# The last two blocks of a chunk-attention and Mish kernel: g @ w_out by seven products of halves, in a phase of its own

## The chip, the cores and the metric

One Trainium2 chip, one of its cores. The metric is the device time of one execution in microseconds; the kernel before took 867.61 us, the median of three runs (866.41 to 867.76).

## The reference

Attention within chunks of 64 tokens, then a feed-forward layer with the Mish function, all in fp32:

```python
q_c = q.reshape(B, H, nc, chunk, D)          # 8, 8, 9, 64, 64; k_c and v_c alike
scores = scale * np.matmul(q_c, k_c.transpose(0, 1, 2, 4, 3))
scores = scores - np.max(scores, axis=-1, keepdims=True)
attn = np.exp(scores)
attn = attn / (np.sum(attn, axis=-1, keepdims=True) + 1e-09)
out = np.matmul(attn, v_c)
...
x = out.transpose(0, 2, 1, 3).reshape(4608, 512)
h = x @ w_in                                  # w_in 512 x 2048
g = h * np.tanh(softplus(h))                  # Mish
return g @ w_out                              # w_out 2048 x 512
```

## The kernel before

Every fp32 matrix operand is split into a high and a low part in the matmul's own format (fp32r), and a product is made of three: high by high, high by low, low by high. gh and gl are the two parts of g, A11 to S4 (in `ops_of`) those of w_in.

The 4,608 tokens go as 512 first tokens, by plain products, and then four blocks of 1,024 (m = 1 to 4; the code's QUADS). In a block the tokens are two sides of 512, and `unit(m, u)` does x @ w_in for 256 columns of w_in (u = 0 to 7), by seven products of halves in place of eight. Each product is 6 matmuls of 512 columns (L697). The sums of halves of x are made ahead by `x_step`, eleven pairs of steps per block. The operands of w_in lie in scratch memory (`wa_u`), one product's 256 KB at a time, and `load_op` fetches the next one into a ring of 5 tiles when a product has used one.

The seven products of a unit give h of both token sides, in PSUM tiles x, y and v. ACT and DVE copy, add and apply Mish. The first side's g is split at once (`g_split`), and its share of g @ w_out is put on a list, `fill`, as single matmuls of 512 columns (L450). `filled(n)` takes n of them off this list between the products, so that PE always has work. The second side's g is kept in `zb`, and `phase_two(m)` multiplies it with w_out behind the eight units: for each of 16 groups f of 128 rows of w_out, ACT casts gh, DVE subtracts gl, and PE does 12 matmuls, one group behind. In the meantime DVE and ACT make the next block's x. The attention of the next block's four pairs of 128-token tiles is laid into the units, a pair to two units.

w_out stays in SBUF, its high part in `wo_h` and its low part in `wo_l`. All instructions stand in the program's order on each engine (a manual schedule), and SP issues nearly all DMAs in that order.

A tile from a pool waits until the pool's buffer is released by all who use the tile before it. `c_p` has one buffer (8 KB per partition); the outputs of a block's sides also go through it.

Of the kernel before, what the change touches and what calls it, by code (L numbers as in the profile page):

```python
# [23 lines left out]
def kernel(  # L24
# [421 lines left out]
    def down_mm(key, f, d, t, n):  # L446
        if f == 0 and n == 0:
            acc[t] = ps_o.tile([P, DM], F32, name=f"o_{key}_{t}", tag=f"o{t}")
        g, w_ = ((d["gl"], wo_h), (d["gh"], wo_l), (d["gh"], wo_h))[n]
        nc.tensor.matmul(  # L450
            acc[t],
            lhsT=g[:, t * P : (t + 1) * P],
            rhs=w_[:, f],
            start=(f == 0 and n == 0),
            stop=(f == NF - 1 and n == 2),
        )
# [223 lines left out]
    wop = []  # L680

    def load_op():
        if len(wop) < len(ops):
            m, u, n = ops[len(wop)]
            t = wop_p.tile([P, 2, 2, P], F32R, name=f"w{m}_{u}_{n}", tag="w")
            nc.sync.dma_start(
                out=t.bitcast(F32).rearrange("p s k c -> p s (k c)"), in_=ops_of[u][:, OPS.index(n)]
            )
            wop.append(t)

    def product(m, u, n, o, start):
        t = wop[((m - 1) * NU + u) * len(PRODUCTS) + n]
        x = [xo[PRODUCTS[n][1]][:, part] for part in range(2)]
        i = 0
        for w_, x_ in ((0, 0), (1, 0), (0, 1)):
            for kt in range(2):
                nc.tensor.matmul(  # L697
                    o,
                    lhsT=t[:, w_, kt],
                    rhs=x[x_][:, kt],  # L700
                    start=(start and i == 0),
                    stop=(i == 5),
                    skip_group_check=not start,
                )
# [8 lines left out]
    for u in range(1, NU):  # L713
        for place, step, n in (
            ((u - 1, 2), s_adds, u),
            ((u - 1, 3), s_hi, u),
            ((u - 1, 4), s_lo, u),
            ((u - 1, 7), s_load, u + 1),
        ):
            BUILDS.setdefault(place, []).append((step, n))  # L720

    def unit(m, u):
        late = m == 1
# [70 lines left out]
        nc.scalar.copy(out=b2, in_=x)  # L794
# [28 lines left out]
    def phase_two(m):  # L823
# [7 lines left out]
        for f in range(NF):  # L831
# [16 lines left out]
            if f == 10 and m + 1 < QUADS:  # L848
                load_qk(first_pair(m + 2))

    with tc.manual_schedule():
# [10 lines left out]
        p = first_pair(QUADS)
        for t, n in enumerate((9, 6, 6, 3)):
            filled(n)
            store("last", (p + 1, p + 3), t, 2)


# [36 lines left out]
```

## Time and profile before

| what | value |
|---|---|
| median of three runs | 867.61 us |
| the profiled execution's own time | 868.13 us |
| its span | 866.0 us |
| PE busy | 823.5 us (95%), 5724 matmuls |
| DVE busy | 433.7 us (50%) |
| ACT busy | 380.9 us (44%) |
| HBM read, written | 108.00 MB, 28.31 MB |
| mean granted clock of PE | 0.987 |

A profile's times are microseconds from the start of the span. PE is the matmul engine, PEld its weight loads, which lie beside the matmuls; DVE is the vector engine, ACT the scalar engine, SP the queue that issues DMAs. A row of the timeline has start, length, engine, line, operation, out<-in, shape and count, and in brackets the idle time before it with what ended it. A row of the groups has the count, the busy time and the mean in ns of one.

### The profile page before, as it was taken

The page shows a single profiled execution, that of the slowest core. Times are in us where ns is not written, and L with a number is a line of the kernel's source. Part 1 is how long each engine was busy: PE and PEld are TensorE (multiplying, and loading weights), DVE is VectorE, ACT ScalarE, POOL GpSimd, SP SyncE. Part 2 cuts the span into 40 slices and gives each one's busy share as a digit, 9 for nine tenths or more (in the row PEclk, how much of TensorE's full clock was granted, in tenths as well). Part 3 has the DMA queues.
Part 4 walks back from the last instruction along what each step waited for, and adds up shares of the span by engine and source line. Part 5 has one row for each costly group of instructions (what it writes and reads, how often), then busy time and mean ns, then how long its engine had stood idle before and what let it go on. Part 6 is the DMA issues. An engine that isn't in the chain of part 4 may idle for free.

```text
span 866.0 us, 14086 instructions
## 1 busy us (share of the span) xinstructions
PE 823.5 (95%) x5724; PEld 669.8 (77%) x5724; DVE 433.7 (50%) x641; ACT 380.9 (44%) x547; POOL 0.7 (0%) x6
## 2 busy tenths in 40 slices
PE   4978989889999999999999999999999999999997
PEld 4757767568888888888888888888888888888885
DVE  6787878646465663343354635524437432223322
ACT  4768775444454453443443425434435232222321
POOL 0000000000000000000000000000000000000000
PEclk9889999999999999999999999999999999999999
DMA  7698774777777502645544216555432064444202
GB/s 279 246 307 313 274 248 161 245 256 251 255 237 250 145 1 84 202 141 173 158 144 110 61 50 208 146 174 156 139 104 50 1 177 126 119 117 131 49 1 50
DMA packets 71216, 137.24 MB, mean 158 GB/s; under 512 B 6896, under 2 KB 18160, under 8 KB 70128
## 3 DMA queue, kind: packets, MB, share of 16 engines
q1 hardware_dynamic: 70224, 135.29, 49.4%
q10 hardware_dynamic: 928, 1.05, 0.4%
q8 instruction: 46, 0.75, 0.3%
q14 instruction: 18, 0.15, 0.0%
HBM read 108.00 MB, written 28.31 MB: 157 GB/s over the span
## 4 chain that ended last, share of the span: by engine, by line
PE 81%; DVE 7%; DMA 5%; ACT 4%; issue 2%; SPq 1%; ACTq 0%; DVEq 0%
PE x L697 19%; PE v L697 10%; PE y L697 5%; DMA wst<-in_w_in 3%; PE av L228 2%; PE pt L296 2%; PE s L228 2%; DVE wc L128 2%; PE o_(1, 1)_0_2751 L450 1%; PE o_(3, 1)_0_5862 L450 1%; PE o_(2, 1)_0_4323 L450 1%; PE o_(4, 0)_1_6270 L450 1%; PE o_(4, 0)_2_6274 L450 1%; PE o_(2, 1)_2_4331 L450 1%; PE o_(1, 1)_1_2755 L450 1%
## 5 line engine op out<-in xcount | busy, mean ns | idle before, releaser
L697 PE MATMUL x<-x_T,w_S 128*128 128x512 f32 x384 | 99.3, 394 | 2.0 <-ACT zb L778 1.0
L438 DVE CAST gh<-z 128x512 fp32r<-128x512 f32 x72 | 30.6, 425 | 136.3 <-PE o_(4, 0)_3_6288 L450 42.1
L431 ACT ACTIVATE zb<-zb 128x512 f32<-128x512 f32 x64 | 40.4, 632 | 116.0 <-DVE zb L709 115.9
L697 PEld LDWEIGHTS x<-x_T,w_S 128*128 128x128 f32 x384 | 71.0, 188 | 18.2 <-ACT zb L778 1.4
L709 DVE TENSOR_TENSOR zb<-v,zb 128x512 f32<-128x512 f32 x64 | 43.9, 685 | 57.4 <-ACT zb L794 57.4
L709 DVE TENSOR_TENSOR z<-y,z 128x512 f32<-128x512 f32 x32 | 22.1, 692 | 89.4 <-PE y L697 89.4
L440 DVE TENSOR_TENSOR gl<-z,gh 128x512 fp32r<-128x512 f32 x80 | 55.4, 693 | 12.0 <-ACT gh L436 9.5
L794 ACT COPY zb<-x 128x512 f32<-128x512 f32 x32 | 18.8, 586 | 83.2 <-PE x L697 83.2
L697 PE MATMUL x<-x_T,w_A 128*128 128x512 f32 x192 | 49.4, 392 | 3.8 <-ACT zb L794 3.8
L697 PE MATMUL x<-x_B,w_A 128*128 128x512 f32 x192 | 50.4, 397 | 0.9 <-DVE x_B L373 0.7
L697 PE MATMUL y<-x_B,w_A 128*128 128x512 f32 x192 | 51.2, 402 | 0.0
L418 PE MATMUL h<-x_first,wi 128*128 128x512 f32 (+1 forms) x204 | 50.0, 399 | 1.0 <-ACT x_first L336 0.7
L697 PE MATMUL v<-x_B,w_S 128*128 128x512 f32 x192 | 49.2, 392 | 1.3 <-DVE zb L709 1.3
L697 PE MATMUL v<-x_T,w_S 128*128 128x512 f32 x192 | 48.9, 390 | 1.0 <-DMA w_S<-wa 1.0
L418 PEld LDWEIGHTS h<-x_first,wi 128*128 128x128 f32 x204 | 38.9, 204 | 9.3 <-ACT x_first L336 0.9
L431 ACT ACTIVATE z<-z 128x512 f32<-128x512 f32 x32 | 20.2, 631 | 58.4 <-DVE z L709 58.4
L697 PEld LDWEIGHTS x<-x_T,w_A 128*128 128x128 f32 x192 | 35.6, 188 | 13.2 <-ACT zb L794 5.9
L697 PEld LDWEIGHTS v<-x_B,w_S 128*128 128x128 f32 x192 | 35.7, 188 | 9.9 <-DVE zb L709 2.6
L697 PEld LDWEIGHTS v<-x_T,w_S 128*128 128x128 f32 x192 | 35.9, 188 | 9.1 <-issue 1.4
L697 PEld LDWEIGHTS x<-x_B,w_A 128*128 128x128 f32 x192 | 35.0, 188 | 8.8 <-DVE x_B L373 1.1
L697 PEld LDWEIGHTS y<-x_B,w_A 128*128 128x128 f32 x192 | 34.6, 188 | 9.1 <-DVE zb L709 1.8
L296 PE MATMUL pt<-ident,p 128*128 128x128 f32 x144 | 20.9, 290 | 13.7 <-DVE p L287 10.4
(296 smaller groups left out, 1726.4 us busy)
## 6 DMA issues: line engine op xcount, KB each, us to landing
w_S<-wa SPq DMA_DIRECT2D x128, 256.0 KB, 2.8
w_A<-wa SPq DMA_DIRECT2D x96, 256.0 KB, 2.8
v<-in_v SPq DMA_DIRECT2D x16, 512.0 KB, 4.9
wa<-a SPq DMA_DIRECT2D x8, 1024.0 KB, 4.8
wst<-in_w_out SPq DMA_DIRECT2D x7, 1024.0 KB, 5.4
wst<-in_w_in SPq DMA_DIRECT2D x6, 1024.0 KB, 6.2
wa<-wi SPq DMA_DIRECT2D x24, 256.0 KB, 4.1
q<-in_q SPq DMA_DIRECT2D x12, 512.0 KB, 4.1
```

Of the source, the lines that this page charges most:

```text
L128: nc.vector.scalar_tensor_tensor(out=c, in0=x, scalar=mask, in1=y, op0=op, op1=ALU.bitwise_or)
L228: nc.tensor.matmul(o[h * CHUNK : (h + 1) * CHUNK, c, t - ts.start, g], lhsT=l[rows, t, 2 * g + h], rhs=r[rows, t, 2 * g + h], start=True, ...
L296: nc.tensor.transpose(out=d["pt", ts.start][:, t - ts.start, g], in_=d["p"][:, t, g].rearrange("p c k -> p (c k)"), identity=ident,)
L418: nc.tensor.matmul(h[:, cols], lhsT=wi[i // 2][:, i % 2, w_, kt], rhs=x[:, x_, kt, cols], start=(n == 0), stop=(n == 3 * NK - 1),)
L431: nc.scalar.activation(out=out_, in_=in_, func=AF.Mish)
L438: nc.vector.tensor_copy(out=d["gh"], in_=z)
L440: nc.vector.tensor_tensor(out=d["gl"], in0=z, in1=d["gh"].bitcast(F32), op=ALU.subtract)
L450: nc.tensor.matmul(acc[t], lhsT=g[:, t * P : (t + 1) * P], rhs=w_[:, f], start=(f == 0 and n == 0), stop=(f == NF - 1 and n == 2),)
L697: nc.tensor.matmul(o, lhsT=t[:, w_, kt], rhs=x[x_][:, kt], start=(start and i == 0), stop=(i == 5), skip_group_check=not start,)
L709: nc.vector.tensor_tensor(out=z, in0=o, in1=z, op=ALU.add)
L794: nc.scalar.copy(out=b2, in_=x)
```

## The change

Blocks 1 and 2 go as before. In blocks 3 and 4 (`BOTH_FROM = 3`) g @ w_out, too, is made of seven products of halves, and no longer fills the gaps of x @ w_in:

- **Up phase**, `up_two(m, n)`: units 2n and 2n+1 are interleaved, product by product, 14 products of 6 matmuls; each unit has its own PSUM tiles x, y and v. The four quarters of g (G11, G12, G21, G22) and S1 stay in SBUF as 128 x 512 fp32 tiles, 40 of them. The attention of the next block is laid between the products at `beside(h)`.
- **Down phase**, `down_all(m)`: 56 steps, types 0 to 6 with 8 units each. `operand(k, u)`, called two steps ahead, makes the type's sum where it has one (S2 = S1 - G11 and S4 = G12 - S2, on DVE, in place), casts gh on ACT and subtracts gl on DVE; gh and gl have three buffers each. A step is 12 matmuls of 256 columns (L1060 of the new kernel). At the end of a type ACT or DVE takes the accumulated tile out, and DVE adds totals for the products that need two. The last block's last two steps are held back and done half by half, and ACT and DVE copy the last half together.
- **Operands of w_out**: made once, in block 2, for eight units: `t_whole` (DVE: high + low), `t_sums` (three on DVE), `t_hi` (ACT), `t_lo` (DVE, with a DMA of 1 MB to `wb_u`), and `t_keep` (three DMAs). `BUILDS_OUT` lays the four steps beside four products in a row; builds 0 to 2 and 5 to 7 start at the beginning of units 1 to 3 and 5 to 7, build 3 and build 4 at the beginning and the middle of unit 4. All builds use the one buffer of `c_p`.
- **Memory**: w_out's two parts become one tile, `wo`. Behind block 2 the rest of its matmuls is done and stored, then the pools of zb, wo, c and ew are closed, and the new tiles take their room. The ring of operands grows by 6 tiles to 11, and holds w_out's operands too.

```diff
+    LOOK, MORE = 5, 6
+    BOTH_FROM = 3
...
+    OPS_OUT = ("W11", "W21", "W22", "T1", "T3", "T4", "T2")
+    TYPES = (
+        ("G11", "W11", "X"),
+        ("G12", "W21", "Y"),
+        ("S2", "T2", "X"),
+        ("S1", "T1", "Z"),
+        ("S3", "T3", "X"),
+        ("S4", "W22", "Z"),
+        ("G22", "T4", "X"),
+    )
...
+    BUILDS_OUT = {}
+    for n, (u, h) in enumerate(((1, 0), (2, 0), (3, 0), (4, 0), (4, 4), (5, 0), (6, 0), (7, 0))):
+        for i, step in enumerate((t_whole, t_sums, t_hi, t_lo)):
+            BUILDS_OUT.setdefault((u, h + i), []).append((step, n))
+        BUILDS_OUT.setdefault((n, 7), []).append((t_keep, n))
...
+    def t_whole(u):
+        t = bld["o"] = c_p.tile([P, 4, 2, 256], F32, name=f"t_{u}", tag="c")
...
+        nc.vector.tensor_tensor(out=whole, in0=hi, in1=lo, op=ALU.add)
...
+    def t_lo(u):
+        t = bld["o"]
+        nc.vector.tensor_tensor(
+            out=t[:, :, 1].bitcast(F32R), in0=t[:, :, 1], in1=t[:, :, 0], op=ALU.subtract
+        )
+        nc.sync.dma_start(out=ops_out[u][:, 3:], in_=t)
...
+    def operand(k, u):
+        name = TYPES[k][0]
+        if name == "S2":
+            G[u, "S2"] = G[u, "G11"]
+            nc.vector.tensor_tensor(out=G[u, "S2"], in0=G[u, "S1"], in1=G[u, "G11"], op=ALU.subtract)
+        if name == "S4":
+            G[u, "S4"] = G[u, "G12"]
+            nc.vector.tensor_tensor(out=G[u, "S4"], in0=G[u, "G12"], in1=G[u, "S2"], op=ALU.subtract)
+        d = {}
+        g = G[u, name]
+        d["gh"] = ew_l.tile([P, TOK], F32R, name=f"gh_{k}_{u}", tag="gh")
+        nc.scalar.copy(out=d["gh"], in_=g)
+        d["gl"] = ew_l.tile([P, TOK], F32R, name=f"gl_{k}_{u}", tag="gl")
+        nc.vector.tensor_tensor(out=d["gl"], in0=g, in1=d["gh"].bitcast(F32), op=ALU.subtract)
+        return d
...
+        ready = [operand(*steps_[0]), operand(*steps_[1])]
...
+        ends = {
+            0: lambda b: keep("P1", banks_["X"], b),
+            1: lambda b: total("P1", banks_["Y"], b, 0, 0),
+            2: lambda b: keep("U2", banks_["X"], b),
+            3: lambda b: keep("P5", banks_["Z"], b),
+            4: lambda b: total("P5", banks_["X"], b, 1, 1),
+            5: lambda b: total("U2", banks_["Z"], b, 0, 1),
+        }
...
+            if i + 2 < len(steps_):
+                ready.append(operand(*steps_[i + 2]))
+            w_ = next_op()
...
+                mine(k, u, ready.pop(0), w_)
+            load_op()
...
+            if i % 2 and todo:
+                todo.pop(0)()
+            if u == NU - 1 and k in ends:
+                for b in range(2):
+                    ends[k](b)
...
+        early.close()
+        more.append(ctx.enter_context(tc.tile_pool(name="wop2", bufs=MORE)))
+        z_p = ctx.enter_context(tc.tile_pool(name="g", bufs=5 * NU))
+        ew_l = ctx.enter_context(tc.tile_pool(name="ew2", bufs=3))
+        ob_p = ctx.enter_context(tc.tile_pool(name="ob", bufs=3))
+        for _ in range(MORE):
+            load_op()
+        for m in range(BOTH_FROM, QUADS + 1):
+            for n in range(NU // 2):
+                up_two(m, n)
+            down_all(m)
```

First place: DVE behind the units of block 3. Before, in phase two: gl_3b_f is the low part of group f of g, x4 and raw belong to block 4's x.

```order
L440 TENSOR_TENSOR gl_3b_6_5965<-zb_3_0_4606,gh_3b_6_5963 128x512
L373 TENSOR_TENSOR x4_B11_5852<-raw_16_5437,x4_B11_5852 128x4x2x64
L373 TENSOR_TENSOR x4_B21_5855<-raw_16_5437,x4_B21_5855 128x4x2x64
L440 TENSOR_TENSOR gl_3b_7_5985<-zb_3_0_4606,gh_3b_7_5983 128x512
L373 TENSOR_TENSOR x4_B22_5878<-raw_17_5961,x4_B22_5878 128x4x2x64
L378 TENSOR_TENSOR raw_16_5437<-raw_17_5961,raw_16_5437 128x4x128
L440 TENSOR_TENSOR gl_3b_8_6004<-zb_3_4_5214,gh_3b_8_6002 128x512
```

Now, where type 2 of the down phase begins: S2 of unit u is written over G11_3_u (L1017), gl_2_u is its low part (L1026), P1 a total (L1079).

```order
L421 TENSOR_TENSOR raw_14_4978<-raw_14_4978,raw_15_5225 128x4x128
L1017 TENSOR_TENSOR G11_3_0_4758<-S1_3_0_4762,G11_3_0_4758 128x512
L1026 TENSOR_TENSOR gl_2_0_6022<-G11_3_0_4758,gh_2_0_6020 128x512
L1017 TENSOR_TENSOR G11_3_1_4773<-S1_3_1_4777,G11_3_1_4773 128x512
L1026 TENSOR_TENSOR gl_2_1_6041<-G11_3_1_4773,gh_2_1_6039 128x512
L416 TENSOR_TENSOR x4_T2_6057<-raw_15_5225,x4_T2_6057 128x4x2x64
L1079 TENSOR_TENSOR P1_3_5903<-Y_3_0_5906,P1_3_5903 128x512
L1079 TENSOR_TENSOR P1_3_5903<-Y_3_1_5907,P1_3_5903 128x512
L1017 TENSOR_TENSOR G11_3_2_5001<-S1_3_2_5005,G11_3_2_5001 128x512
L1026 TENSOR_TENSOR gl_2_2_6069<-G11_3_2_5001,gh_2_2_6067 128x512
L1017 TENSOR_TENSOR G11_3_3_5016<-S1_3_3_5020,G11_3_3_5016 128x512
```

Between one gl and the next there now stands the sum that ACT's cast for that next gl reads; type 5 has the same rows with L1020, and block 4 the same without the x4 and raw rows.

Second place: DVE at the end of unit 4 of block 2. Before: zb and z are additions behind products (L709), p and r belong to the attention.

```order
L282 RECIPROCAL r_12_0_3776<-r_12_0_3776 128x16
L709 TENSOR_TENSOR zb_2_4_3675<-v_2_4_3759,zb_2_4_3675 128x512
L287 TENSOR_TENSOR p_12_3743<-p_12_3743,r_12_0_3776 128x2x8x64
L438 CAST gh_2_9_3818<-z_2_9_3805 128x512
L440 TENSOR_TENSOR gl_2_9_3820<-z_2_9_3805,gh_2_9_3818 128x512
L709 TENSOR_TENSOR zb_2_4_3675<-v_2_4_3759,zb_2_4_3675 128x512
L709 TENSOR_TENSOR z_2_10_3835<-y_2_5_3849,z_2_10_3835 128x512
```

Now: t_4 and t_5 are builds 4 and 5, L210 is `t_whole`, L219 `t_sums`, L227 `t_lo`, and L776 the additions that were L709. The next row behind these is the addition z_2_10<-y_2_5.

```order
L210 TENSOR_TENSOR t_4_3834<-wo_98 128x4x256
L776 TENSOR_TENSOR zb_2_4_3721<-v_2_4_3813,zb_2_4_3721 128x512
L330 TENSOR_TENSOR p_12_3794<-p_12_3794,r_12_0_3830 128x2x8x64
L219 TENSOR_TENSOR t_4_3834<-t_4_3834 128x2x256
L219 TENSOR_TENSOR t_4_3834<-t_4_3834 128x256 x2
L481 CAST gh_2_9_3878<-z_2_9_3864 128x512
L483 TENSOR_TENSOR gl_2_9_3880<-z_2_9_3864,gh_2_9_3878 128x512
L776 TENSOR_TENSOR zb_2_4_3721<-v_2_4_3813,zb_2_4_3721 128x512
L227 TENSOR_TENSOR t_4_3834<-t_4_3834 128x4x256
L210 TENSOR_TENSOR t_5_3901<-wo_98 128x4x256
L219 TENSOR_TENSOR t_5_3901<-t_5_3901 128x2x256
L219 TENSOR_TENSOR t_5_3901<-t_5_3901 128x256 x2
```

`t_whole` of build 4 now stands ahead of the first addition of zb, and `t_lo` of build 4 and the whole beginning of build 5 ahead of the addition of z.

More of the change, by code (lines that the diff above doesn't have):

```diff
@@ L678, with next_op, product @@
     OPS = ("A11", "A12", "A22", "S2", "S4", "S3", "S1")
-    ops = [(m, u, n) for m in range(1, QUADS + 1) for u in range(NU) for n, _ in PRODUCTS]
+    OPS_OUT = ("W11", "W21", "W22", "T1", "T3", "T4", "T2")
[7 more added lines that the diff above has]
+        ("G22", "T4", "X"),
+    )
+    ops = [
+        (m, ops_of, u, OPS.index(n)) for m in range(1, BOTH_FROM) for u in range(NU) for n, _ in PRODUCTS
+    ]
+    few = len(ops)
+    for m in range(BOTH_FROM, QUADS + 1):
+        for u in range(0, NU, 2):
+            ops += [(m, ops_of, u + i, OPS.index(n)) for n, _ in PRODUCTS for i in range(2)]
+        ops += [(m, ops_out, u, OPS_OUT.index(n)) for _, n, _ in TYPES for u in range(NU)]
     wop = []
+    used = []
+    more = []
     def load_op():
[L683 to L688, printed above, removed]
-            wop.append(t)
-    def product(m, u, n, o, start):
-        t = wop[((m - 1) * NU + u) * len(PRODUCTS) + n]
+        n = len(wop)
+        if n < len(ops):
+            m, src, u, place = ops[n]
+            pool = wop_p if n < few or (n - few) % (LOOK + MORE) < LOOK else more[0]
+            t = pool.tile([P, 2, 256], F32R, name=f"w{n}", tag="w")
+            nc.sync.dma_start(out=t.bitcast(F32), in_=src[u][:, place])
+            wop.append(t)
+    def next_op():
+        used.append(0)
+        return wop[len(used) - 1]
+    def product(n, o, start):
+        t = next_op().rearrange("p s (k c) -> p s k c", k=2)
         x = [xo[PRODUCTS[n][1]][:, part] for part in range(2)]
@@ L733, in beside @@
                 run(BUILDS, (u, n))
+            if m == BOTH_FROM - 1:
+                run(BUILDS_OUT, (u, n))
         beside(0)
@@ L807, in unit @@
         beside(6)
-        product(m, u, 6, y, False)
+        product(6, y, False)
         filled()
@@ L849, in phase_two, with bank, z_new, flip @@
                 load_qk(first_pair(m + 2))
+    OPEN = (("h", "h"), ("o0", "o1"), ("o2", "o3"))
+    G = {}
+    def bank(name, tag):
+        return (ps_h if tag == "h" else ps_o).tile([P, TOK], F32, name=name, tag=tag)
+    def z_new(m, u, name):
+        G[u, name] = z_p.tile([P, TOK], F32, name=f"{name}_{m}_{u}", tag="z")
+        return G[u, name]
+    def flip(m):
+        return OPEN if (m - BOTH_FROM) % 2 == 0 else (OPEN[0], OPEN[2], OPEN[1])
+    def s_sums(u):
+        s1, g11, g21, g22 = (G[u, n] for n in ("S1", "G11", "G21", "G22"))
+        nc.vector.tensor_tensor(out=s1, in0=g21, in1=g22, op=ALU.add)
+        nc.vector.tensor_tensor(out=g21, in0=g11, in1=g21, op=ALU.subtract)
+        G[u, "S3"] = g21
@@ new lines, in up_two, with beside @@
+    def up_two(m, n):
+        units = (2 * n, 2 * n + 1)
+        xt, yt, vt = flip(m)
+        j = first_pair(m + 1) + n
+        on = m < QUADS
+        x, y, v_ = {}, {}, {}
+        def beside(h):
+            if h in (1, 2) and n:
+                s_sums(2 * n - 3 + h)
+            if not on:
+                return
+            if h == 1:
+                a_scores(j)
+                load_v(j)
+            elif h == 2:
+                a_max(j)
+            elif h == 3:
+                a_sub(j)
+                if n < 3:
+                    load_qk(j + 1, pool=(ob_p, "ob"))
+            elif h == 4:
+                a_exp(j)
+            elif h == 6:
+                a_inverse(j)
+            elif h == 7:
+                a_norm(j)
+            elif h == 9:
+                a_transpose(j)
+                a_copy(j)
+            elif h == 11 and n < 3:
+                a_values(j)
+                a_raw(j)
+        for k in range(7):
+            for i, u in enumerate(units):
+                if k == 0:
+                    x[u] = bank(f"x_{m}_{u}", xt[i])
+                    z11 = z_new(m, u, "G11")
+                    for name in ("G12", "G21", "G22", "S1"):
+                        z_new(m, u, name)
+                if k == 1:
+                    y[u] = bank(f"y_{m}_{u}", yt[i])
+                if k == 3:
+                    v_[u] = bank(f"v_{m}_{u}", vt[i])
+                o = y[u] if k == 1 else v_[u] if k in (3, 6) else x[u]
+                product(k, o, k in (0, 1, 3))
+                z = {name: G[u, name] for name in ("G11", "G12", "G21", "G22")}
+                if k == 0:
+                    nc.scalar.copy(out=z["G11"], in_=o)
+                elif k == 1:
+                    add(o, z["G11"])
+                    mish(z["G11"], z["G11"])
+                elif k == 2:
+                    nc.scalar.copy(out=z["G21"], in_=o)
+                elif k == 4:
+                    nc.scalar.copy(out=z["G22"], in_=o)
+                    add(v_[u], z["G22"])
+                    mish(z["G22"], z["G22"])
+                elif k == 5:
+                    mish(z["G12"], o)
+                elif k == 6:
+                    add(o, z["G21"])
+                    mish(z["G21"], z["G21"])
+                beside(2 * k + i)
@@ L861 @@
         by_token()
[L862 to L865, printed above, removed]
+        p = first_pair(BOTH_FROM - 1)
+        key = f"{BOTH_FROM - 1}b"
+        for t in range(TOK // P):
+            filled(3)
+            store(key, (p + 1, p + 3), t)
+        early.close()
[5 more added lines that the diff above has]
+            load_op()
+        for m in range(BOTH_FROM, QUADS + 1):
+            for n in range(NU // 2):
+                up_two(m, n)
+            down_all(m)
 def kernel(q, k, v, moe_w_in, moe_w_out):
```

130 lines of the change are left out of this document (113 added, 17 removed).

## Prediction

> **What bounds the kernel now.** I read the page first: which engine is busy, at what clock, and which engine carries the chain that ended last.
>
> ```profile
> span 866.0 us, 14086 instructions
> ...
> PE 823.5 (95%) x5724; PEld 669.8 (77%) x5724; DVE 433.7 (50%) x641; ACT 380.9 (44%) x547; POOL 0.7 (0%) x6
> ...
> PEclk9889999999999999999999999999999999999999
> ...
> PE 81%; DVE 7%; DMA 5%; ACT 4%; issue 2%; SPq 1%; ACTq 0%; DVEq 0%
> ```
>
> PE is the bound and its clock is full for almost the whole span. Next the table of windows, one stretch each for blocks 2, 3 and 4:
>
> ```profile
> 336.00:514.00 178.00, 177.78 (x1266) 145.81 (x1265) 80.99 (x122) 74.62 (x110) 0.00 (x0) 1.00 0.44 131
> 514.00:692.00 178.00, 177.78 (x1265) 145.83 (x1264) 81.00 (x122) 74.62 (x110) 0.00 (x0) 1.00 0.43 125
> 692.00:860.00 168.00, 167.40 (x731) 136.21 (x729) 48.26 (x78) 46.19 (x79) 0.00 (x0) 1.00 0.35 95
> ```
>
> The columns are length, busy time of PE, weight load (PEld), DVE, ACT and POOL, then clock, DMA share and GB/s. In each block PE idles 0.2 to 0.6 us, while DVE and ACT are busy under half the time. So only two things change the time: how much matmul time there is, and any wait that PE does not have today. The change takes matmul time away and adds serial work on DVE and ACT, and I weigh the two.
>
> **The matmuls.** The timeline early in the run has the only 256-column matmuls of this kernel (12, with their loads), and a full-clock run of twelve 512-column ones:
>
> ```profile
> 16.93 1.69 PE L418 MATMUL h<-x_first,wi 128*128 128x256 f32 x12
> ...
> 16.92 1.49 PEld L418 LDWEIGHTS h<-x_first,wi 128*128 128x128 f32 x12
> ...
> 39.14 2.88 PE L418 MATMUL h<-x_first,wi 128*128 128x512 f32 x12
> ```
>
> Durations overlap, so the distance between starts counts. For 512 columns, with one matmul at 0.39 us, it is (2.88 - 0.39)/11 = 0.226 us. For 256 columns the loads step by (1.49 - 0.19)/11 = 0.118. The matmul row gives (1.69 - 0.28)/11 = 0.128, but holds a cold first pair. I take 0.118, with 0.128 as the upper bound. A 512-token half of g @ w_out was 16 x 4 x 3 matmuls, so a block had 384 x 0.226 = 86.9 us. Now it has 7 x 8 x 4 x 3 = 672 x 0.118 = 79.4 (0.128: 86.1). That is 7.5 us less per block, **-15.0** for two. A step of twelve matmuls takes 12 x 0.118 = 1.42 us. The up phase keeps its 336 products of 512 columns.
>
> The Trainium skill (TensorE: Matmul & The Clock Gate, section Back-to-back issue gap) gives N/2.4 + 2.5 ns; by it this term would be 2 x (672 x 0.109 - 384 x 0.216) = -19.4, an estimate from that page, but the trace's steps are about 10 ns longer at both widths.
>
> **The new serial chain, S2 and S4.** In the new down phase each step needs a cast gh on ACT and a subtraction gl on DVE. For types S2 and S4 (8 steps each) a DVE subtraction makes the operand first. By the order, DVE has S2 of step i, gl of step i, S2 of step i+1, and gl needs ACT's cast of that S2. The prices are in phase two of block 3, and the handovers in block 2:
>
> ```profile
> 673.36 0.69 DVE L440 TENSOR_TENSOR gl_3b<-zb,gh_3b 128x512 fp32r<-128x512 f32 x1 [0.70 <-ACT gh_3b L436]
> 673.97 0.69 DVE L378 TENSOR_TENSOR raw<-raw,raw 128x512 f32<-128x512 f32 x1
> 674.58 0.69 DVE L373 TENSOR_TENSOR x_T<-raw,x_T 128x512 fp32r<-128x512 f32 x1
> ...
> 683.59 0.62 ACT L436 CAST gh_3b<-zb 128x512 fp32r<-128x512 f32 x1 [2.10 <-PE o_(3, 1)_3_5874 L450]
> ...
> 684.24 0.69 DVE L440 TENSOR_TENSOR gl_3b<-zb,gh_3b 128x512 fp32r<-128x512 f32 x1 [2.03 <-ACT gh_3b L436]
> ...
> 429.31 0.59 ACT L794 COPY zb<-x 128x512 f32<-128x512 f32 x1 [3.95 <-PE x L697]
> 429.93 0.69 DVE L709 TENSOR_TENSOR zb<-v,zb 128x512 f32<-128x512 f32 x1 [3.02 <-ACT zb L794]
> 430.65 0.63 ACT L431 ACTIVATE zb<-zb 128x512 f32<-128x512 f32 x1 [0.76 <-DVE zb L709]
> ```
>
> A DVE operation of this size takes 0.69 us and the next independent one starts 0.61 after it; a handover between ACT and DVE costs 0.03. One turn of the chain is 0.69 + 0.03 + 0.62 + 0.03 + 0.61 = 1.98 us, against PE's 1.42. PE has little ahead: three buffers of gh and gl, so two steps.
>
> Take time 0 as PE's due start of the first S2 step, in block 4. Step -1's cast waits for the buffer of step -4, whose matmuls end at -4.10 (-3 x 1.42, and 0.28 - 0.12 for the last one's own end). So gl of step -1 ends at -4.10 + 0.03 + 0.62 + 0.03 + 0.69 = -2.73, and S2 of step 0 starts at -2.81. Its gl ends at -0.75, gl of step 1 at 1.23. Then DVE adds two totals for the product that has just ended (2 x 0.61), so S2 of step 2 starts at 2.37 and its gl ends at 4.43. From there one per 1.98: step 7 at 14.33, where PE is due at 7 x 1.42 = 9.94. PE loses 4.4 us. The S4 steps have the same rows, so block 4 loses 8.8. In block 3 four instructions of the next block's x operands stand in the same stretch, 4 x 0.61 = 2.4 us more, twice: 13.6. Together **+22.4**, and I take it. Bounds: 8 us less if DVE enters each of the four stretches a turn ahead, 4 us more if it enters half a turn late.
>
> **The border between the phases.** Before, g @ w_out filled PE while DVE and ACT finished a unit. Now, behind the last product of x @ w_in, PE has nothing: add 0.69, mish 0.63, the first cast 0.62 (behind the mish on ACT), gl 0.69, and four handovers of 0.03. That is 2.75 us, **+5.6** for two blocks. From block 3 to 4 and from 2 to 3 PE has products ready, at no cost; without that cover it would be another 2.8 each.
>
> **Building w_out's operands in block 2.** All 8 builds share one buffer. Most are a unit apart and DVE has room. Two are not: build 4 starts one step behind the end of build 3, and build 5 right behind build 4, so DVE stands at t_whole until the 1 MB store has landed, with what PE waits for queued behind it.
>
> ```profile
> 407.04 1.23 DVE L266 TENSOR_TENSOR p<-s,m 128x1024 f32<-128x1024 f32 x1
> ...
> 412.06 0.25 DVE L282 RECIPROCAL r<-r 128x16 f32<-128x16 f32 x1
> 412.75 0.69 DVE L709 TENSOR_TENSOR zb<-v,zb 128x512 f32<-128x512 f32 x1 [0.44 <-ACT zb L794]
> 413.36 1.22 DVE L287 TENSOR_TENSOR p<-p,r 128x1024 f32<-128x1024 f32 x1
> ...
> 414.43 0.39 PE L697 MATMUL v<-x_B,w_S 128*128 128x512 f32 x1
> ...
> 417.81 0.68 DVE L709 TENSOR_TENSOR zb<-v,zb 128x512 f32<-128x512 f32 x1
> ...
> 425.48 0.84 PE L697 MATMUL v<-x_T,w_S 128*128 128x512 f32 x3
> ...
> L193 DVE TENSOR_TENSOR a<-a 128x1024 fp32r<-128x1024 f32 x8 | 9.6, 1199 | 0.2
> ...
> L185 DVE TENSOR_TENSOR a<-a 128x256 f32<-128x256 f32 x32 | 13.6, 424 | 12.1 <-DMA a<-cs 11.2
> ```
>
> and the DMA view, with the KB of one and the time to landing:
>
> ```profile
> wa<-a SPq DMA_DIRECT2D x8, 1024.0 KB, 4.8
> wst<-in_w_in SPq DMA_DIRECT2D x6, 1024.0 KB, 6.2
> ...
> cs<-wc SPq DMA_DIRECT2D x6, 512.0 KB, 2.8
> ```
>
> In the times of before: t_lo of build 3 follows p at 408.3 and ends at 409.5; the store lands 4.8 later, 414.3; t_whole (1.2) and the add of zb end at 416.1, and the product v that accumulates on what this add reads was due at 414.43: 1.7 us. In unit 5: t_lo of build 4 ends 1.2 behind the add at 417.81, so at 421.3 with the delay; landing 426.2; t_whole, three sums (0.69 + 0.42 + 0.42) and the add of z end at 429.6; the product v that needs its bank was due at 425.48 + 1.7 = 427.2: 2.4 us. **+4.1**. With 2.8 us for the store (half the size) it is 0.6, with 6.2 (a load) 6.9.
>
> **The end.** Before, the last matmul starts at 859.32, and a copy that waited its turn ends at 861.85, before the last DMA:
>
> ```profile
> 859.32 0.39 PE L450 MATMUL o_(4, 1)_3_7019<-wo_h,gh_4b 128*128 128x512 f32 x1
> ...
> 861.48 0.37 ACT L497 COPY ob_last<-o_(4, 1)_3_7019 128x256 f32<-128x256 f32 x1 [1.19 <-DVE ob_last L495]
> 861.88 1.13 ACTq L501 DMA_DIRECT2D out<-ob_last  x2
> ```
>
> Now ACT and DVE copy one half each (0.4) right behind the last matmul (0.28), so the DMA starts 0.7 instead of 2.5 us behind it: **-1.8** (0 if the larger last transfer takes it back).
>
> **The stream.** Up and down phases read one 256 KB operand per 1.36 or 1.42 us, some 190 GB/s, and block 3 reads 5 MB of q, k and v beside. Eleven buffers are 15 us ahead:
>
> ```profile
> DMA packets 71216, 137.24 MB, mean 158 GB/s; under 512 B 6896, under 2 KB 18160, under 8 KB 70128
> ...
> 71.50:74.90 3.40, 3.40 (x75) 2.67 (x74) 2.76 (x3) 2.90 (x4) 0.00 (x0) 1.00 0.99 287
> ```
>
> In that window, the last number, the queues reached 287 GB/s at a share of 0.99; asked are some 245 (190, and 5 MB over the 178 - 86.9 = 91 us of an up phase). So it is hidden and costs nothing.
>
> **Sum.** -15.0 + 22.4 + 5.6 + 4.1 - 1.8 = +15.3 us. The profiled execution took 868.1 (span 866.0 and 2.1 around it), 0.5 above the median of 867.6; on the median the sum gives **882.9 us**, 1.8% slower.
>
> **The rivals.** *The chain stays hidden, and the kernel is faster.* If S2 and S4 ran while DVE waits for ACT, a step would cost DVE 2 x 0.61 = 1.22 us, under 1.42, and the 22.4 would go: -7.1, 860.5 us. The turning point is a turn of 1.42. For it: DVE is idle half the span. Against it: the order, and the rows at 412.06 to 413.36: p needed only r, ready at 412.31, but DVE stood 0.44 for zb and took p behind it. 9 in 100. The Trainium skill (TensorE: Matmul & The Clock Gate, section Architectural detail) says that of the engines only PE pulls work ahead and ACT and DVE are strict queues; by that rule this rival is out, and these rows agree.
>
> *The clock falls in the new gaps.* After a window in which PE was nearly idle the trace shows the clock at half for 3.4 us, after one with 1.7 us idle it does not:
>
> ```profile
> 64.60:68.10 3.50, 0.46 (x29) 0.46 (x32) 1.96 (x3) 3.49 (x4) 0.00 (x0) 1.00 0.69 281
> 68.10:71.50 3.40, 3.40 (x54) 2.82 (x46) 1.11 (x1) 2.15 (x3) 0.00 (x0) 0.50 0.41 161
> ...
> 180.80:184.20 3.40, 1.66 (x6) 1.05 (x6) 3.33 (x7) 1.93 (x3) 0.00 (x0) 1.00 0.10 37
> 184.20:187.60 3.40, 3.34 (x19) 2.86 (x20) 1.99 (x4) 1.12 (x2) 0.00 (x0) 1.00 0.75 308
> ```
>
> A gap of 2.75 us can fill most of a window. Each fall costs 3.4/2 = 1.7 us; four of them give 890. 13 in 100. The Trainium skill (same page, section Why this matters for your kernels) warns of idle gaps above about 3 us; by it these gaps just pass.
>
> *The loads set the pace*: 672 x 0.19 = 127.7 per block and no wait for the chain, 2 x (127.7 - 86.9) + 5.6 + 4.1 - 1.8 = +89.5, 957 us. The loads 0.118 apart speak against it. 1 in 100. *The stream is late*, so that the change does not do what it says: at the mean of 158 GB/s an operand takes 1.66 us, 0.26 x 224 = +58, 941 us; 287 reached speaks against it. 3 in 100.
>
> **How the numbers follow.** My forecast has 72 in 100, the clock 13, the hidden chain 9, the stream 3, the loads 1; 2 are left for sums that cancel. About 0.2% (1.7 us) is what a measurement of this kernel can tell. Faster 0.09, same 0.02, slower 0.89. Range: down to 873 (8 less in the chain, 2 in the builds), up to 893 (6.7 x 40/56 x 2 = 9.6 for 0.128 us a matmul, or the clock).
>
> **What would show it.** In the profile after: 256-column matmuls 0.118 apart; in types 2 and 5 a gl on DVE every 1.98 us, and PE waiting for gl, 4 to 7 us in each of four stretches; a gap of 2.8 us at each border from up to down; t_whole waiting for a DMA in units 4 and 5 of block 2. The forecast is wrong if PE stays closed in types 2 and 5, or if it waits for DMA.

## The result, and the profile after

The kernel after takes 892.88 us (median of four runs, 891.89 to 898.4), the kernel before 867.68 beside it: a ratio of 1.030 (95% interval 1.0252 to 1.0348). The forecast was slower, 882.9 us in 873 to 893. The direction came, but 10 us more than forecast, at the very top of the range: the ratio measured side by side is 1.030, and 893/867.61 is 1.029. The page of the kernel after, from a run of 893.57 us:

```profile
span 891.8 us, 15840 instructions
...
PE 823.5 (92%) x6300; PEld 693.1 (78%) x6300; DVE 525.3 (59%) x765; ACT 437.1 (49%) x640; POOL 0.7 (0%) x6
...
PE 64%; DVE 17%; ACT 9%; DMA 5%; issue 3%; SPq 1%; ACTq 0%; DVEq 0%
...
L1026 DVE TENSOR_TENSOR gl<-G,gh 128x512 fp32r<-128x512 f32 x96 | 65.8, 692 | 59.7 <-ACT gh L1024 58.6
...
L1060 PE MATMUL X<-w,gl 128*128 128x256 f32 x256 | 75.5, 295 | 14.6 <-DVE gl L1026 14.6
...
w<-wb SPq DMA_DIRECT2D x112, 256.0 KB, 2.8
```

PE's busy time is what it was, 823.5 us, although matmul work went: a matmul at half clock (0.58 us, below) and the first one behind each wait (0.39 for 0.28) take longer. The last run below has the same 6,300 matmuls and almost none of these waits, and its PE is busy for 812.4 us. PE has fallen from 81 to 64% of the chain that ended last, DVE has risen from 7 to 17%, ACT from 4 to 9%. PE waits for gl, and gl for ACT's cast. The windows of the kernel after, one row each for up and down of block 3 and up and down of block 4 (length, busy PE, PEld, DVE, ACT, POOL, clock, DMA share, GB/s):

```profile
520.33:614.03 93.70, 90.12 (x817) 72.36 (x815) 44.18 (x60) 52.28 (x75) 0.00 (x0) 1.00 0.76 236
616.88:713.88 97.00, 86.85 (x736) 83.90 (x737) 66.17 (x103) 44.43 (x76) 0.00 (x0) 0.98 0.59 164
713.88:790.53 76.65, 76.65 (x338) 62.59 (x336) 24.08 (x36) 31.60 (x56) 0.00 (x0) 1.00 0.70 199
793.38:886.96 93.58, 86.52 (x672) 84.04 (x672) 53.24 (x81) 36.69 (x61) 0.00 (x0) 0.97 0.53 144
```

The up phase of block 4 is closed. That of block 3, which has the attention beside it, idles 3.6 us; the down phases idle 10.2 and 7.1, and between the rows lie the borders. No DMA is waited for in them. Now the four places in turn.

**S2 and S4.** The timeline of the kernel after, type 2 of block 4, DVE and ACT rows:

```profile
823.10 0.69 DVE L1026 TENSOR_TENSOR gl<-G,gh 128x512 fp32r<-128x512 f32 x1 [0.76 <-ACT gh L1024]
823.71 0.68 DVE L1017 TENSOR_TENSOR G<-S,G 128x512 f32<-128x512 f32 x1
825.16 0.69 DVE L1026 TENSOR_TENSOR gl<-G,gh 128x512 fp32r<-128x512 f32 x1 [0.76 <-ACT gh L1024]
...
824.50 0.62 ACT L1024 CAST gh<-G 128x512 fp32r<-128x512 f32 x1 [1.44 <-DVE G L1017]
```

From gl to gl it is 2.06 us: 0.61 to the sum's start, 0.68 for it, 0.11 to the cast (823.71 + 0.68 = 824.39, cast at 824.50), 0.62 for that, 0.04, and gl again. The forecast had 0.03 for the handover that is 0.11, hence 1.98. By the starts of the matmuls a step of PE is 1.44, eight are 11.52, and the four stretches took 18.87, 19.16, 16.73 and 16.46: a loss of 7.35 + 7.64 + 5.21 + 4.94 = 25.1.

**Builds.** DVE and PE rows of the kernel after, units 4 and 5 of block 2:

```profile
413.78 1.23 DVE L210 TENSOR_TENSOR t<-wo 128x1024 f32<-128x1024 f32 x1 [1.57 <-DMA wb<-t]
...
425.20 1.22 DVE L210 TENSOR_TENSOR t<-wo 128x1024 f32<-128x1024 f32 x1 [4.14 <-DMA wb<-t]
...
415.66 1.67 PE L764 MATMUL v<-x_B,w 128*128 128x512 f32 x6 [1.18 <-DVE zb L776]
428.73 1.67 PE L764 MATMUL v<-x_T,w 128*128 128x512 f32 x6 [1.69 <-DVE z L776]
```

The waits are where they were forecast, but 1.2 and 1.7 us long where 1.7 and 2.4 were forecast. With smaller ones beside them, block 3's first product starts at 520.33, 4.1 us later than the kernel before's times give (513.51, and twelve matmuls of 0.227 that now stand ahead of it: 516.23). Block 2 by itself lost 4.8: it starts at 334.76 in the kernel after and at 335.46 in the kernel before, so it takes 185.57 in place of 180.77, and an earlier start of 0.7 hides part of that.

**Attention beside the up phase of block 3.** DVE, ACT and PE rows of the first of the four pairs:

```profile
551.02 1.22 DVE L297 TENSOR_REDUCE m<-s 128x16 f32<-128x1024 f32 x1
552.16 0.68 DVE L776 TENSOR_TENSOR G<-y,G 128x512 f32<-128x512 f32 x1
...
558.18 1.23 DVE L330 TENSOR_TENSOR p<-p,r 128x1024 f32<-128x1024 f32 x1
...
552.87 0.63 ACT L474 ACTIVATE G<-G 128x512 f32<-128x512 f32 x1 [2.42 <-DVE G L776]
...
554.05 1.28 ACT L318 ACT_TABLE_LOAD   x1
555.34 1.06 ACT L318 ACTIVATE p<-p 128x1024 f32<-128x1024 f32 x1
...
559.56 1.07 PE L339 MATMUL pt<-ident,p 128*128 128x128 f32 x8 [0.98 <-DVE p L330]
```

An addition of g stands behind the maximum on DVE; its mish, a copy and a table load go ahead of the exponential on ACT; so PE, due to transpose, stands 0.98 us for the division on DVE. It happens three times, and with smaller waits costs 3.7 us. No step of the prediction had it. The same pair in the kernel before, PE and DVE rows:

```profile
546.92 1.16 PE L228 MATMUL s<-k,q 64*64 64x64 f32 x64
...
557.96 1.22 DVE L287 TENSOR_TENSOR p<-p,r 128x1024 f32<-128x1024 f32 x1
...
561.07 1.03 PE L296 MATMUL pt<-ident,p 128*128 128x128 f32 x8
```

From the end of the scores (548.08) to the transposes PE had 13.0 us of matmuls, 36 of the products and 21 from `fill`, and the division ended 11.1 us behind the scores. Now the scores end at 547.39, 48 matmuls of the products last until 558.58, which is 11.2 us, and the division ends at 559.41, 12.0 us behind the scores. So the cover lost 1.8 us and the chain gained 0.9.

**Borders and clock.** PE rows at the two borders, then windows around them and in type 5 of block 3:

```profile
616.88 0.39 PE L1060 MATMUL X<-w,gl 128*128 128x256 f32 x1 [2.68 <-DVE gl L1026]
...
793.38 0.58 PE L1060 MATMUL X<-w,gl 128*128 128x256 f32 x1 [2.68 <-DVE gl L1026]
```

```profile
615.20:618.60 3.40, 1.72 (x14) 1.73 (x15) 2.47 (x4) 1.94 (x4) 0.00 (x0) 1.00 0.28 80
686.90:690.30 3.40, 1.25 (x10) 1.25 (x11) 1.94 (x4) 1.21 (x3) 0.00 (x0) 1.00 0.68 156
690.30:693.70 3.40, 3.29 (x16) 2.99 (x15) 2.58 (x5) 1.17 (x3) 0.00 (x0) 0.50 0.74 226
789.30:792.70 3.40, 1.40 (x7) 0.82 (x5) 1.46 (x3) 1.87 (x4) 0.00 (x0) 1.00 0.62 189
792.70:796.10 3.40, 2.73 (x12) 2.73 (x13) 3.37 (x6) 0.94 (x2) 0.00 (x0) 0.50 0.10 37
```

Both gaps are 2.68 us, as forecast. Behind the second the clock is at half for 6.8 us, and the first eight steps of block 4 take 14.31 us in place of 11.52: 2.8 more. Behind the first it stays full. Both gaps lie over an edge between two windows of the clock, which cuts the first into 1.0 and 1.7 us and the second into 2.0 and 0.7 (the windows are worked out at the end).

The last matmul starts at 886.84, 4.96 us from the end of the span (6.68 before): -1.7. Term by term (0.227 is the mean distance of the 512-column matmuls' starts in blocks 3 and 4 of the kernel before):

| term | forecast us | measured us |
|---|---|---|
| matmuls, 0.120 apart (672 x 0.120 for 384 x 0.227, twice) | -15.0 | -13.1 |
| S2 and S4 | +22.4 | +25.1 |
| borders (2 x 2.68) | +5.6 | +5.4 |
| half clock behind the second border | 0 | +2.8 |
| builds, by the length of block 2 | +4.1 | +4.8 |
| earlier start of block 2 | 0 | -0.7 |
| attention beside up 3; up 4 (76.65 for 336 x 0.227) | 0 | +3.7; +0.4 |
| end | -1.8 | -1.7 |
| not put down to a row | | -0.9 |
| sum (the two spans) | +15.3 | +25.8 |

### The profile page after: what moved, and what is told of

It reads as the page before. It is cut to its first block, busy times and chain, and to the rows that moved or that the text cites. A ratio compares the mean times of both kernels' runs of the same rounds, so it can differ in the third digit from the quotient of the medians.

```text
span 891.8 us, 15840 instructions
## 1 busy us (share of the span) xinstructions
PE 823.5 (92%) x6300; PEld 693.1 (78%) x6300; DVE 525.3 (59%) x765; ACT 437.1 (49%) x640; POOL 0.7 (0%) x6
## 4 chain that ended last, share of the span: by engine, by line
PE 64%; DVE 17%; ACT 9%; DMA 5%; issue 3%; SPq 1%; ACTq 0%; DVEq 0%
PE x L764 15%; PE v L764 8%; PE X L1060 8%; PE y L764 4%; PE Z L1060 3%; DVE gl L1026 3%; ACT gh L1024 2%; DMA wst<-in_w_in 2%; PE av L271 2%; PE Y L1060 2%; DVE wc L132 2%; PE s L271 2%; PE pt L339 2%; PE o_(1, 1)_0_2761 L493 1%; PE o_(2, 1)_0_4421 L493 1%
## 5 line engine op out<-in xcount | busy, mean ns | idle before, releaser
L764 PE MATMUL x<-x_T,w 128*128 128x512 f32 x576 | 144.8, 394 | 5.9 <-ACT zb L868 3.3
L764 PEld LDWEIGHTS x<-x_T,w 128*128 128x128 f32 x576 | 106.1, 188 | 32.3 <-ACT zb L868 4.6
L1024 ACT CAST gh<-G 128x512 fp32r<-128x512 f32 x96 | 58.9, 619 | 96.0 <-PE X L1060 30.6
L1026 DVE TENSOR_TENSOR gl<-G,gh 128x512 fp32r<-128x512 f32 x96 | 65.8, 692 | 59.7 <-ACT gh L1024 58.6
L1060 PE MATMUL X<-w,gh 128*128 128x256 f32 x512 | 95.4, 287 | 0.0
L1060 PE MATMUL X<-w,gl 128*128 128x256 f32 x256 | 75.5, 295 | 14.6 <-DVE gl L1026 14.6
L1060 PEld LDWEIGHTS X<-w,gh 128*128 128x128 f32 x512 | 81.9, 197 | 0.0
L1060 PEld LDWEIGHTS X<-w,gl 128*128 128x128 f32 x256 | 50.3, 196 | 18.1 <-DVE gl L1026 18.1
L776 DVE TENSOR_TENSOR G<-v,G 128x512 f32<-128x512 f32 x32 | 22.1, 691 | 65.8 <-ACT G L1003 34.7
L764 PE MATMUL x<-x_B,w 128*128 128x512 f32 x192 | 48.6, 394 | 0.8 <-DVE x_B L416 0.8
L764 PE MATMUL y<-x_B,w 128*128 128x512 f32 x192 | 49.1, 397 | 0.0
L1060 PE MATMUL Z<-w,gh 128*128 128x256 f32 x256 | 47.9, 287 | 0.0
L1060 PE MATMUL Z<-w,gl 128*128 128x256 f32 x128 | 38.3, 299 | 8.0 <-DVE gl L1026 7.9
```

What stands on the lines that cost most here:

```text
L764: nc.tensor.matmul(o, lhsT=t[:, w_, kt], rhs=x[x_][:, kt], start=(start and i == 0), stop=(i == 5), skip_group_check=not start,)
L776: nc.vector.tensor_tensor(out=z, in0=o, in1=z, op=ALU.add)
L1024: nc.scalar.copy(out=d["gh"], in_=g)
L1026: nc.vector.tensor_tensor(out=d["gl"], in0=g, in1=d["gh"].bitcast(F32), op=ALU.subtract)
L1060: nc.tensor.matmul(o, lhsT=d[g][:, t * P : (t + 1) * P], rhs=w_[:, part], start=(k in (0, 1, 3) and u == 0 and t % 2 == 0 and n == 0), sto ...
```

## The experiments

Theory: the loss is the four waits above, each from the order of a few instructions, and without them the change is a gain. Rivals stand in the expectations. Each time is a median, beside runs of the kernel before whose median was 868.2 or 867.8; a gain is against the 892.88 of the kernel after, which was not measured again beside them. A diff is against the kernel after.

**The sums made a type earlier.**

```diff
     def operand(k, u):
         name = TYPES[k][0]
-        if name == "S2":
-            G[u, "S2"] = G[u, "G11"]
-            nc.vector.tensor_tensor(out=G[u, "S2"], in0=G[u, "S1"], in1=G[u, "G11"], op=ALU.subtract)
-        if name == "S4":
...
         nc.vector.tensor_tensor(out=d["gl"], in0=g, in1=d["gh"].bitcast(F32), op=ALU.subtract)
+        if name == "G12":
+            G[u, "S2"] = G[u, "G11"]
+            nc.vector.tensor_tensor(out=G[u, "S2"], in0=G[u, "S1"], in1=G[u, "G11"], op=ALU.subtract)
+        if name == "S1":
...
```

> The sums S2 and S4 are made earlier, S2 eight steps ahead behind the low part of G12, S4 sixteen steps ahead behind the low part of S1; nothing else moves, and DVE does as many operations as before. Theory (the serial turn sum, cast, low part on DVE and ACT closes PE in types 2 and 5): all steps of these types take 1.44 us, the four stretches lose under 1 us each in place of 7.3, 7.6, 5.2 and 4.9, and the kernel takes 892.9 - 25 = 868 us (865 to 871). Rival (DVE has too much to do in the down phase, whatever the order): the waits move to the types that now hold the sums, and the kernel stays above 885 us.

Measured 867.31 us, ratio 0.9982 (0.9970 to 0.9993): 25.6 less, at the level of the kernel before. All four stretches (types 2 and 5 of blocks 3 and 4) are 11.52 us long, 25.1 us less in all; of the other types, 3 and 4 of block 3 are 0.07 and 0.09 longer. The half clock now falls behind the first border and not the second, and both types 0 together take 1.1 us less. Its timeline in type 1 of block 4, DVE:

```profile
799.25 0.69 DVE L1020 TENSOR_TENSOR gl<-G,gh 128x512 fp32r<-128x512 f32 x1
799.85 0.68 DVE L1023 TENSOR_TENSOR G<-S,G 128x512 f32<-128x512 f32 x1
800.68 0.69 DVE L1020 TENSOR_TENSOR gl<-G,gh 128x512 fp32r<-128x512 f32 x1
...
802.13 0.69 DVE L1020 TENSOR_TENSOR gl<-G,gh 128x512 fp32r<-128x512 f32 x1 [0.75 <-ACT gh L1018]
```

The same 32 subtractions are done on the same engine, but the cast of the next step doesn't read them, so gl comes every 1.43 to 1.45 us. This shows that the order and not the work cost the 25 us.

**The cast of S2 and S4 on DVE.**

```diff
-        nc.scalar.copy(out=d["gh"], in_=g)
+        if name in ("S2", "S4"):
+            nc.vector.tensor_copy(out=d["gh"], in_=g)
+        else:
+            nc.scalar.copy(out=d["gh"], in_=g)
```

> In types 2 and 5 DVE makes gh itself, so a turn has no handover and no ACT work in it. Theory (one turn of sum, cast and gl is what PE waits for): in the kernel after, a turn is 2.06 us (0.61 + 0.12 + 0.61 + 0.03 + 0.69). With DVE's own cast (0.42 us, the next instruction 0.46 behind its start, as in L481 of block 2) it is 0.61 + 0.46 + 0.61 = 1.68 against PE's 1.44. A stretch of eight steps loses 7 x 0.24 = 1.7 in place of 7 x 0.62 = 4.3, so about 2.3 in block 4 where it was 5.0, and 4.8 in block 3 where it was 7.5: 11 us less in all, about 882. Rival (DVE's amount of work is the limit, not the order): 32 more DVE instructions of 0.46 us make it 15 us longer, about 907.

Measured 886.39 us (1.0207, 1.0181 to 1.0234), 6.5 less: more work on DVE and yet faster, so the amount of work was not the bound. But the size was off. DVE rows of block 4, type 2:

```profile
819.49 0.68 DVE L1017 TENSOR_TENSOR G<-S,G 128x512 f32<-128x512 f32 x1
820.28 0.43 DVE L1025 CAST gh<-G 128x512 fp32r<-128x512 f32 x1
820.74 0.69 DVE L1029 TENSOR_TENSOR gl<-G,gh 128x512 fp32r<-128x512 f32 x1
821.35 0.68 DVE L1017 TENSOR_TENSOR G<-S,G 128x512 f32<-128x512 f32 x1
```

A turn is 1.86 us, not 1.68: the cast reads what the sum writes, and starts 0.79 behind its start, not 0.61. The 0.61 holds between independent operations only. The stretches took 17.20, 17.22, 14.81 and 14.81.

**A fourth buffer.**

```diff
-    LOOK, MORE = 5, 6
+    LOOK, MORE = 5, 4
...
-        ew_l = ctx.enter_context(tc.tile_pool(name="ew2", bufs=3))
+        ew_l = ctx.enter_context(tc.tile_pool(name="ew2", bufs=4))
```

> gh and gl have four buffers in place of three (the ring of operands shrinks from 11 to 9 tiles to make room). Theory (a serial turn of 2.06 us against a step of 1.44 sets the pace): one more buffer lets the chain enter a stretch at most one step, 1.44 us, earlier; the turn stays at 2.06. At most 4 x 1.44 = 5.8 us less, 887 to 892. Rival (the turn is long because casts wait for the buffer that PE frees): with a fourth buffer the turn falls to 1.44 and most of the 25 us goes, 868 to 875. A wait of PE for the DMA of an operand would show that the shorter ring is late.

Measured 887.35 us (1.0230, 1.0200 to 1.0260), 5.5 less where at most 5.8 was expected. The turn stays at 2.05 to 2.06, and each stretch is 1.4 to 1.7 us shorter (17.43, 17.43, 15.02, 15.03; 6.3 us together): about a step's lead, used up once per stretch. PE doesn't wait for an operand's DMA, with 9 tiles in the ring either.

**The first operands ahead of the last product.**

```diff
+    first = []
...
         for k in range(7):
+            if k == 6 and n == 3:
+                first[:] = [operand(0, 0), operand(0, 1)]
...
-        ready = [operand(*steps_[0]), operand(*steps_[1])]
+        ready = list(first)
```

> The casts and low parts of the first two steps of the down phase are issued ahead of the last two products of the up phase. Theory (the gaps of 2.7 us at the two borders, and the half clock that follows the second one, 2.8 us): both gaps under 0.5 us, no half clock behind the border of block 4, 892.9 - 8.2 = 884.7 us. Rival (the gap only moves two steps on, since the third step's cast stands behind the same mish): under 3 us of gain, 890 us or more, with a gap of 1 us or more at the third step.

Measured 888.43 us (1.0228, 1.0206 to 1.0251), 4.5 less where 8.2 was expected. Both gaps at the border are gone, but at the fourth step PE waits, 0.98 us in block 3 and 1.56 in block 4. The timeline there, block 4:

```profile
788.69 0.69 DVE L1029 TENSOR_TENSOR gl<-G,gh 128x512 fp32r<-128x512 f32 x1 [1.21 <-ACT gh L1027]
789.30 0.68 DVE L944 TENSOR_TENSOR S<-G,G 128x512 f32<-128x512 f32 x1
...
791.95 1.89 DVE L1029 TENSOR_TENSOR gl<-G,gh 128x512 fp32r<-128x512 f32 x3
...
792.69 0.39 PE L1063 MATMUL X<-w,gl 128*128 128x256 f32 x1 [1.56 <-DVE gl L1029]
```

Its gl stands behind the four sums of units 6 and 7 (`s_sums`). ACT's cast for it had ended at 789.17, so the wait is DVE's order and not the cast. In the kernel after the gap of 2.68 had hidden that. The next run moves them (this diff is against the run just shown):

```diff
-                first[:] = [operand(0, 0), operand(0, 1)]
+                first[:] = [operand(0, f) for f in range(3)]
...
-            if i == 1:
-                for u_ in (NU - 2, NU - 1):
-                    s_sums(u_)
-            if i + 2 < len(steps_):
+            if i in (4, 6):
+                s_sums(NU - 4 + i // 2)
+            if 0 < i < len(steps_) - 2:
```

> As e2_border_covered, but three operands in place of two are made ahead of the last product of the up phase, and the four sums for units 6 and 7 stand at steps 4 and 6 of the down phase in place of all at step 1. Theory (what was left in e2_border_covered, 0.98 and 1.56 us at the fourth step, came from gl of that step standing behind these four sums on DVE): both gaps go, the border costs nothing, about 885 to 886. Rival (the cast of that step is late on ACT, behind the last mish): the gaps stay at the fourth step, 888.

Measured 884.46 us (1.0187, 1.0161 to 1.0213), 8.4 less: the border with its half clock is the 8.2 of the table's two rows. Both waits are gone; in block 4 the first eight steps take 11.51 us.

**Builds 3 and 4 a phase apart.**

```diff
-    for n, (u, h) in enumerate(((1, 0), (2, 0), (3, 0), (4, 0), (4, 4), (5, 0), (6, 0), (7, 0))):
+    for n, (u, h) in enumerate(((1, 0), (2, 0), (3, 0), (4, 0), (8, 0), (5, 0), (6, 0), (7, 0))):
...
+            if m == BOTH_FROM - 1 and f in (9, 10, 11, 12):
+                run(BUILDS_OUT, (8, f - 9))
```

> Build 4 of w_out's operands moves from the middle of unit 4 of block 2 to phase two of block 2, groups 9 to 12. Theory (DVE stood for the store of the build before in the one shared buffer): PE's waits of 1.2 and 1.7 us in units 4 and 5 go, block 3 starts 4.2 us earlier, 888.7 us. Rival (DVE is simply full there, the builds cost wherever they are): phase two shows 2 us or more of PE waits instead, and the time stays within 2 us of 892.9.

Measured 888.0 us (1.0243, 1.0208 to 1.0278), 4.9 less. PE has no wait left in units 4 and 5, nor in phase two, and block 3 starts at 513.78, 6.5 us earlier. Of that, 2.2 is an earlier start of block 2 in this run (332.57); block 2 itself takes 181.2 us in place of 185.6. Some of it went back: the clock now fell behind both borders, for 3.4 and 6.8 us.

**The transposes a product later.**

```diff
-            elif h == 9:
+            elif h == 10:
                 a_transpose(j)
...
-            elif h == 11 and n < 3:
+            elif h == 12 and n < 3:
```

> In the up phase of block 3 the transposes of the attention stand one product later, and the products with v one product later too. Theory (the chain scores, maximum, exp, norm is 1 us longer than the products laid over it, three times): the three waits of 0.98 us ahead of the transposes go, block 3's up phase takes 90 in place of 93.7 us, 889.4 us. Rival (the chain moves with it, ACT's copy of the transposes or the product with v is late next): the up phase takes 92.5 us or more.

Measured 890.23 us (1.0249, 1.0229 to 1.0268), 2.7 less. The three waits of 0.98 are gone, and a wait of 0.36 us appears three times in front of the next product, which waits for an ACT copy. The up phase of block 3 takes 91.25 us where it took 93.7.

**All four.** The sums a type earlier, the border as in the second form, the builds and the transposes.

> The four edits together: sums S2 and S4 made behind gl of types 1 and 3, the first three operands of the down phase made ahead of the last product of the up phase (with the sums of units 6 and 7 two steps apart, at steps 4 and 6), build 4 in phase two, transposes one product later. Theory (the losses add, and without them only the saving in matmul time and the end are left): 892.9 - 25.1 (chain) - 8.2 (borders and the half clock behind the second) - 4.8 (builds) - 2.5 (attention) = about 852, which is 15 to 16 below the kernel before. Rival (in block 3 DVE then has gl, the next sum and half an x instruction per step of type 1, 0.61 + 0.61 + 0.3 = 1.52 us against a step of 1.44, and the losses come back there): 8 to 10 us more in types 1 and 3 of block 3 and at the borders, 860 or above.

Measured 854.43 us (851.92 to 857.49), ratio 0.9846 (0.9821 to 0.9872): 13.4 faster than the kernel before, 38.5 faster than the kernel after. About 852 was expected; one by one the four gains were 41.6. The page and the same four windows as above:

```profile
span 852.3 us, 15846 instructions
...
PE 812.4 (95%) x6300; PEld 688.9 (81%) x6300; DVE 522.4 (61%) x765; ACT 437.3 (51%) x640; POOL 0.7 (0%) x6
...
PE 78%; DVE 9%; ACT 5%; DMA 5%; issue 2%; SPq 1%; ACTq 0%; DVEq 0%
```

```profile
515.67:606.88 91.21, 90.09 (x817) 72.66 (x815) 43.93 (x60) 52.49 (x77) 0.00 (x0) 1.00 0.77 243
606.88:690.20 83.32, 83.18 (x737) 82.20 (x737) 66.03 (x106) 46.11 (x79) 0.00 (x0) 1.00 0.67 196
690.20:766.85 76.65, 76.65 (x339) 62.76 (x337) 24.71 (x38) 32.72 (x58) 0.00 (x0) 1.00 0.70 199
766.85:847.36 80.51, 80.51 (x672) 80.51 (x671) 53.37 (x82) 37.79 (x62) 0.00 (x0) 1.00 0.60 174
```

PE is closed again in three of the four, to within 0.2 us. In the last row 672 matmuls take 80.51 us, 0.120 each, with DVE busy as long as in the kernel after (53.4 against 53.2). The rival of a DVE too full in type 1 of block 3 is there, but small: by the starts of its matmuls that type takes 12.04 in place of 11.52, 0.13 more in every second step, where PE stands for gl. The busy time doesn't show waits this short. What is left of the table is the matmuls and the end, -14.8, and 13.4 was measured.

## Why the prediction was right in direction and 10 us short

The path was right: the loss lies where PE waits for DVE and ACT. Three steps of the prediction failed. "The up phase keeps its 336 products of 512 columns" put that phase at nothing, and it cost 4.1 us. The clock stood at nothing in the sum, and it cost 2.8. The turn of the new chain was sized 1.98 us and is 2.06, which is most of 2.7 us. The matmuls' saving was 1.9 us smaller than forecast.

- **The bound: right.** Block 4's up phase is closed, and the down phases lose where PE waits for DVE and ACT.
- **S2 and S4: right in mechanism, 2.7 short.** The step that failed is the sum of the turn, "0.69 + 0.03 + 0.62 + 0.03 + 0.61 = 1.98": the handover behind the sum is 0.11, so it is 2.06. Eight such turns in each of four stretches make 2.6 us, less 0.6 because PE's own step is 1.44 and not 1.42; the last 0.7 is not put down to a row. Making the sums earlier gave back 25.6. The rival of a hidden chain came true only when the order was changed.
- **The matmuls: 1.9 short.** The step was 0.118 from the loads of one stretch of twelve and 0.226 from one of 512 columns; over 672 it is 0.120, and the 512 ones are 0.227.
- **"The up phase keeps its 336 products of 512 columns"** failed by what it left out. It counted PE's work and not what stands beside it: the attention's chain lost the single matmuls that had covered it (13.0 us of cover before, 11.2 now) and has itself become 0.9 us longer. That cost 3.7 us in block 3, of which the later transposes gave 2.7 back.
- **The half clock, 2.8: a rival that came beside the forecast.** The prediction set the limit between a window with almost no PE work and one with 1.7 us idle. The limit lies right behind that second row. It priced a fall at 1.7; the border's took 2.8, for two windows. The Trainium skill (TensorE: Matmul & The Clock Gate, section Why this matters for your kernels) warns of gaps above about 3 us; here 2.68 us was enough, and the measurement decides.
- **Builds: right in mechanism, and in size by luck.** The two waits were 1.2 us shorter together than forecast. Smaller ones more than made up for it, so block 2 by itself lost 4.8, and its earlier start took 0.7 of that off again. Moving build 4 gave back 4.4 of the 4.8.
- **Borders, end and stream: right** within 0.2 us each. PE's waits in the stretches are for gl and none for DMA; the time to landing of w_out's operands is 2.8 us, with eleven tiles ahead.
- **-0.9 us** of the table is not put down to a row; half of it is 0.5 us of PE's waits in blocks 3 and 4 of the kernel before.

## What to carry to other kernels

When a change takes covering work from PE, walk each chain that the cover hid, instruction by instruction in the engines' order, and price it as a turn against PE's step. Here an operand whose making needs DVE, ACT and DVE again cost 25 us when it was begun two steps ahead of its use, and nothing when its sum was made eight or sixteen steps earlier; what lies between was not tried. An independent DVE operation costs its spacing (0.61 us here), a dependent one its whole length and the handover (0.71 to 0.79). And a kernel that is slower may hold a gain: here 38.5 us of waits and half clock lay on top of 13.
